# The first load of a decode kernel, split by rows: 16 rows in a load of their own, 112 behind them

## The chip, the core and the metric

The kernel runs on one core of a Trainium2 chip. The metric is the device time of one execution in microseconds, as the median of several runs: 697.33 us before the change.

## What is computed

A gated mix of two branches for one decode step: two sequences (B = 2), one token each, width D = 640. Branch a is attention over a cached K and V (32 heads, 4096 positions, 128 wide, float32), branch b a feed-forward network.

```python
def _A_ref(x, k_cache, v_cache, wq, wo):
    q = (x @ wq).reshape(B, Sq, H, Dh).transpose(0, 2, 1, 3)
    scores = einsum("bhqd,bhkd->bhqk", q, k_cache) * (Dh ** -0.5)
    p = softmax(scores, axis=-1)
    o = einsum("bhqk,bhkd->bhqd", p, v_cache)
    return o.transpose(0, 2, 1, 3).reshape(B, Sq, H * Dh) @ wo

def _B_ref(x, w1, w2):
    return silu(x @ w1) @ w2

g = sigmoid((x * gate_w).sum(-1, keepdims=True))
return g * a + (1 - g) * b
```

Everything is float32. Nearly all of the bytes are the two caches: 16 pieces of K and 16 of V, 8.39 MB each, of 298.26 MB that are read in all.

## The kernel before

**Tiling.** The 32 heads are taken four at a time, for each of the two sequences: 8 x 2 = 16 items (`items`). One item's K, and likewise its V, is 128 partitions x 16,384 floats (`SLAB`), so 65,536 bytes in each partition. Three buffers of that size hold everything big: slab a, slab b and slab v. K goes to b and a in turn (`kslab`), V to slab v, the last V to slab b.

**Per item.** VectorE and GpSimd multiply K by the query (L607 and L601), VectorE sums the products to scores (L617) and finds the peak, ScalarE takes the exponentials (L646), TensorE multiplies them with V (L697) and gathers the rows (L745).

**The start.** The queries come first. wq, 640 x 4096, is viewed as 128 rows of 20,480 floats (`wq_rows`, L274): each partition holds five rows of wq. Four of the five, 16,384 floats, go to slab a with the first load (L275), which is the load that the change touches; the fifth goes to slab v (L279). Two small loads bring x and the gate weights on ScalarE's queue (L277, L278). w1 follows into slab v (L280), and then the first K into slab b (`load_k(0)`, L286). `mm_qr` (L398) multiplies x by slab a and then by the rest in slab v. When it has read slab a, the second K is loaded into it (`load_k(1)`), and when w1 has been read, the first V into slab v.

**What sets the order.** The program is written down once as a list of operations. `Flow.dma` (L66) records a load on the queue of SP or ACT, with keys that say which part of a buffer it writes, and a semaphore of its own. `part("a")` stands for the eight keys a.0 to a.7 of slab a. An operation that reads a key waits for the last one that wrote it (`Flow.op`, L40). Loads on one queue are issued in the order in which they are recorded; in the profile they all have line L68, so they are told apart by buffer and source ("slab_a<-in_A_wq_dram" is the first load). A load waits at its issue until the readers of its buffer are done. The first four of SP's loads wait for nothing but the start.

**The end.** wo, in eight pieces of 1.31 MB, is multiplied with the attention rows (L533), two of them and w2 halfway through the items, the other six last, into slab v. The two partial sums are merged (L546, L551), copied (L841) and stored.

Of the kernel before, what the change touches and what calls it, by code (L numbers as in the profile page):

```python
# [142 lines left out]
def gated_decode(nc, x, kc, vc, wq, wo, w1, w2, gate, out):  # L143
# [14 lines left out]
    SLAB = C * DH  # L158
# [8 lines left out]
    N = len(items)  # L167
    MID = 5
    LOOPED = N - 2

    f = Flow(nc)
    V, S_, T_, G_ = nc.vector, nc.scalar, nc.tensor, nc.gpsimd

    def sb(name, shape, align=32):
        return nc.alloc_sbuf_tensor(name, shape, F32, align_bytes=align)[tuple([slice(None)] * len(shape))]
# [6 lines left out]
    slab = {n: sb(f"slab_{n}", [P, SLAB], 512) for n in "abv"}  # L182

    def part(n, *ks):
        return [f"{n}.{k}" for k in (ks or range(8))]
# [69 lines left out]
    def load_v(i):  # L255
        src = run_of(vflat, i)
        if i < N - 1:
            v_load[i] = f.dma("SP", slab["v"], src, writes=part("v"), signal=h_v if i < LOOPED else None)
            return
# [5 lines left out]
    def load_wo(grp, n, key, after):  # L265
# [6 lines left out]


    wq_rows = wq.rearrange("(p j) n -> p (j n)", j=J)  # L274
    f.dma("SP", slab["a"], wq_rows[:, :SLAB], writes=part("a"))  # L275
    xg = slab["v"][: B + 1, XG_AT : XG_AT + D]
    f.dma("ACT", xg[:B], x.rearrange("b s d -> (b s) d"), writes=part("v", 6))  # L277
    f.dma("ACT", xg[B : B + 1], gate[None, :], writes=part("v", 7))  # L278
# [5 lines left out]
        writes=part("v", 1, 2, 3, 4, 5),  # L284
# [10 lines left out]
        writes=["ident"],  # L295
# [8 lines left out]
    for q in range(Q):  # L304
# [3 lines left out]
            writes=["fold"] if q == 0 else [f"fold{q}"],  # L308
# [6 lines left out]
        writes=["sel"],  # L315
# [5 lines left out]
        writes=["half"],  # L321
# [6 lines left out]
        writes=["pick"],  # L328
# [5 lines left out]
        writes=["own"],  # L334
    )
    for q in range(Q):
# [6 lines left out]
            writes=[f"spread{q}"],  # L343
# [19 lines left out]
    for b in range(B):  # L363
# [4 lines left out]
            writes=[f"gx{b}"],  # L368
# [6 lines left out]
        writes=["ps_o"],  # L375
# [8 lines left out]
        writes=["gc"],  # L384
# [59 lines left out]
    for u in range(2):  # L444
# [10 lines left out]
            writes=[f"ps_{u}"],  # L455
# [29 lines left out]
    for src, key, k, dst, dkey, e in (  # L485
# [9 lines left out]
            writes=["turned"],  # L495
# [9 lines left out]
            writes=[ek],  # L505
# [5 lines left out]
            writes=[dkey],  # L511
        )
    for e in range(2):
# [4 lines left out]
            writes=[f"hTh{e}"],  # L518
# [93 lines left out]
    def scores(i):  # L612
        k = slab[kslab(i)].rearrange("p (c d) -> p c d", d=DH)
        for n, (c0, c1) in enumerate(((0, CV), (CV, C))):
            ops["scores", i] = f.op(
                "DVE",
                lambda c0=c0, c1=c1: V.reduce_sum(Ss[i % 2][:, c0:c1], k[:, c0:c1, :], axis=AX.X),  # L617
                reads=part(kslab(i), n),
                writes=[f"s{i % 2}{n}"],
            )  # L620
# [19 lines left out]
    def weights(i):  # L640
        s = Ss[i % 2]

        def fn():
# [16 lines left out]
            writes=["pz", "rs"],  # L660
            signal=h_e if i < LOOPED else None,
        )

    def relay(i):
        ops["relay", i] = f.op("ACT", lambda: S_.sem_inc(h_q), after=[ops["scores", i]], signal=None)
        ops["relay", i].signal = "sent"
# [59 lines left out]
    def combine(i):  # L726
# [11 lines left out]
            writes=["osb"],  # L738
            signal=h_o if i < LOOPED else None,
        )  # L740
# [37 lines left out]
    for i in range(N + 1):  # L778
        j = i - 1
        loop = j if 0 <= j < LOOPED else None  # L780

# [11 lines left out]
        if i < N:  # L793
            scores(i)
            if 1 <= i <= LOOPED:
                relay(i)
# [4 lines left out]
        if i == MID:  # L801
            after = f.users(part("a"))
            for grp in range(WO_MID):
# [5 lines left out]
                writes=part("a", 2),  # L809
# [6 lines left out]
                writes=part("a", 3),  # L816
# [72 lines left out]
```

## Time and profile before

| | |
|---|---|
| median of three runs | 697.33 us (697.23 to 697.35) |
| the profiled execution | 697.66 us |
| its span, first to last instruction | 695.7 us |
| outside the span | 1.96 us |
| bytes read | 298.26 MB, 429 GB/s over the span |
| granted TensorE clock, mean | 0.674 |

In the profile PE is TensorE's matmuls, PEld its weight loads, DVE VectorE, ACT ScalarE, POOL GpSimd, SP the sync engine, whose queue issues the big loads; "SPq" is that queue. q1 is the DMA queue of SP's loads and q10 that of ScalarE's. The DMA row gives the mean busy share of the core's 16 DMA engines in each of 40 slices, and the row below it what they moved. In a table of stretches, each row has the stretch, its length, the busy time of PE, PEld, DVE, ACT and POOL with their instruction counts, the granted clock of TensorE, the DMA share and the rate in GB/s. A packet is counted whole in the stretch in which it starts.

### The profile page before, as it was taken

Reading aid. Unit: us, or ns where it says so; the run is one execution under the profiler, and the core shown is the slowest. Engines: PE = TensorE matmul, PEld = TensorE weight load, DVE = VectorE, ACT = ScalarE, POOL = GpSimd, SP = SyncE. Lnnn points to the kernel's source line nnn. Section 1 sums busy time; section 2 is a strip of 40 time slices with the busy share of each in tenths; the row PEclk is TensorE's granted clock in tenths of the full one; section 3 lists DMA queues with packets and bytes.
Section 4 is the critical chain, followed back from the end, with each engine's and each line's share of the span. In section 5 each row is a group of like instructions: output and inputs, shape, how many; then the busy total and the mean of one; then the engine's idle time right before and its main releaser. Section 6 shows DMA issues by size and latency. Waiting matters only on the chain. (4 is left out here: it accounts for less than half of the span.)

```text
span 695.7 us, 3701 instructions
## 1 busy us (share of the span) xinstructions
PE 223.3 (32%) x1520; PEld 88.2 (13%) x1520; DVE 478.8 (69%) x235; ACT 40.1 (6%) x153; POOL 264.9 (38%) x26
## 2 busy tenths in 40 slices
PE   1630042240506053542150606041240606050377
PEld 1110011010102011110020302010120303020012
DVE  1016998969688695194949678594949588695930
ACT  0010001010101001001010101001010101001010
POOL 1006391808080624502709071533518080624400
PEclk9985556575757567877575757566575757566599
DMA  9999999999999999999999999999999999999997
GB/s 400 413 460 426 426 423 452 438 426 433 422 448 441 426 433 414 455 427 433 426 452 430 430 433 426 452 430 430 430 430 452 433 430 426 430 460 426 413 419 304
DMA packets 6938, 298.38 MB, mean 429 GB/s; under 512 B 775, under 2 KB 911, under 8 KB 1170
## 3 DMA queue, kind: packets, MB, share of 16 engines
q1 hardware_dynamic: 6924, 298.26, 99.2%
q8 instruction: 5, 0.08, 0.0%
q14 instruction: 3, 0.02, 0.0%
q10 hardware_dynamic: 6, 0.01, 0.0%
HBM read 298.26 MB, written 0.01 MB: 429 GB/s over the span
## 5 line engine op out<-in xcount | busy, mean ns | idle before, releaser
L697 PE MATMUL ps<-slab_v,pz 128*32 128x512 f32 x960 | 140.3, 745 | 352.6 <-PEq L129 326.2
L601 POOL TENSOR_TENSOR slab_b<-slab_b,qsb 128x7680 f32<-128x7680 f32 x8 | 131.4, 16421 | 204.1 <-DMA slab_b<-in_A_k_cache_dram 189.2
L601 POOL TENSOR_TENSOR slab_a<-slab_a,qsb 128x7680 f32<-128x7680 f32 x8 | 131.5, 16433 | 182.3 <-DMA slab_a<-in_A_k_cache_dram 168.9
L617 DVE TENSOR_REDUCE s<-slab_b 128x68 f32<-128x8704 f32 (+1 forms) x16 | 138.2, 8676 | 0.0
L617 DVE TENSOR_REDUCE s<-slab_a 128x68 f32<-128x8704 f32 (+1 forms) x16 | 138.1, 8675 | 0.0
L607 DVE TENSOR_TENSOR slab_b<-slab_b,ps 128x8704 f32<-128x8704 f32 x8 | 73.7, 9216 | 51.4 <-DMA slab_b<-in_A_k_cache_dram 51.4
L697 PEld LDWEIGHTS ps<-slab_v,pz 128*32 128x32 f32 x960 | 52.3, 133 | 428.2 <-issue 401.0
L607 DVE TENSOR_TENSOR slab_a<-slab_a,ps 128x8704 f32<-128x8704 f32 x8 | 73.8, 9221 | 46.5 <-DMA slab_a<-in_A_k_cache_dram 44.1
L646 ACT ACTIVATE pz<-s,nb 32x128 f32<-32x128 f32 x64 | 25.5, 398 | 581.5 <-PE ps L697 448.9
L745 PE MATMUL ps<-osb,pick 128*128 128x512 f32 x32 | 18.6, 663 | 26.9 <-PEq L129 25.1
L729 DVE SCALAR_TENSOR_TENSOR osb<-ps,rg,own 128x512 f32<-128x512 f32 x16 | 12.0, 750 | 21.0 <-PE ps L697 20.9
L757 DVE TENSOR_REDUCE row<-ps 128x128 f32<-128x512 f32 x16 | 11.1, 691 | 21.3 <-PE ps L745 21.3
L493 DVE STREAM_TRANSPOSE turned<-ps 128x416 f32<-128x416 f32 (+1 forms) x2 | 0.8, 416 | 28.4 <-PE ps L475 28.3
L418 PE MATMUL ps<-qall,spread 128*128 (+1 forms) x32 | 6.9, 300 | 25.3 <-DVE slab_b L607 24.5
L683 DVE RECIPROCAL ps<-ps 128x1 f32<-128x1 f32 x16 | 2.7, 168 | 16.4 <-PE ps L671 16.4
L533 PE MATMUL ps<-slab_v,oP 128*17 128x320 f32 (+2 forms) x128 | 12.0, 368 | 2.1 <-DMA slab_v<-in_A_wo_dram 2.1
L671 PE MATMUL ps<-rs,fold 128*128 128x1 f32 x32 | 6.0, 257 | 19.9 <-PEq L129 19.7
L398 PE MATMUL ps<-slab_a,xz 128*32 128x512 f32 x64 | 9.1, 732 | 9.3 <-DMA slab_a<-in_A_wq_dram 9.3
L646 ACT ACTIVATION_READ_ACCUMULATOR pz<-s,nb 32x1 f32 x64 | 11.8, 184 | 0.0
L533 PE MATMUL ps<-slab_a,hT 128*17 128x320 f32 x52 | 8.9, 509 | 7.0 <-DMA slab_a<-in_B_w_dram 7.0
L418 PEld LDWEIGHTS ps<-qall,spread 128*128 128x128 f32 x32 | 6.4, 206 | 33.5 <-DVE slab_b L607 24.7
L745 PEld LDWEIGHTS ps<-osb,pick 128*128 128x128 f32 x32 | 5.0, 195 | 41.1 <-issue 37.4
(70 smaller groups left out, 94.1 us busy)
## 6 DMA issues: line engine op xcount, KB each, us to landing
slab_v<-in_A_wo_dram SPq DMA_DIRECT2D x5, 1280.0 KB, 18.1
slab_v<-in_B_w_dram SPq DMA_DIRECT2D x1, 4320.0 KB, 37.3
slab_a<-in_B_w_dram SPq DMA_DIRECT2D x1, 4160.0 KB, 26.8
slab_b<-in_A_v_cache_dram SPq DMA_DIRECT2D x1, 4096.0 KB, 38.2
slab_b<-in_A_v_cache_dram SPq DMA_DIRECT2D x2, 2048.0 KB, 44.8
slab_a<-in_A_wo_dram SPq DMA_DIRECT2D x2, 1280.0 KB, 16.1
slab_v<-in_A_wq_dram SPq DMA_DIRECT2D x1, 2048.0 KB, 26.9
slab_v<-in_A_wo_dram SPq DMA_DIRECT2D x1, 960.0 KB, 25.1
```

Source lines behind the costliest of these rows:

```text
L398: last = T_.matmul(qr[u][32 * q : 32 * q + 32, :], xz[:, j, :], w[:, u * HALF : (u + 1) * HALF, q, :], start=(j == 0), stop=(j == J - 1),)
L418: return T_.matmul(ps_q[:, :DH], spread, qall.rearrange("p h b d -> p (h b) d")[:, i, :], start=True, stop=True,)
L533: last = T_.matmul(dst[32 * n : 32 * n + m, :], lhsT, w[:, n * width : (n + 1) * width], start=first, stop=final,)
L601: lambda: G_.tensor_mul(k[:, CV:, :], k[:, CV:, :], qsb[:, None, :].to_broadcast([P, C - CV, DH])),
L607: lambda: V.tensor_mul(k[:, :CV, :], k[:, :CV, :], ps_q[:, None, :DH].to_broadcast([P, CV, DH])),
L617: lambda c0=c0, c1=c1: V.reduce_sum(Ss[i % 2][:, c0:c1], k[:, c0:c1, :], axis=AX.X),
L646: last = S_.activation(pz[lo:hi, :, 4 * q : 4 * q + 4], s[lo:hi].rearrange("p (g c) -> p g c", c=4), AF.Exp, bias=nb[lo:hi], scale=SCALE, ...
L671: lambda *_: T_.matmul(ps_t[:, :1], fold.rearrange("p a q c -> p (a q c)"), rs, start=True, stop=True),
L697: last = T_.matmul(ps_v[32 * q : 32 * q + 32, :], pz[:, gr, :], v[:, gr, :], start=(gr < 4), stop=(gr >= NG - 4),)
L729: lambda: V.scalar_tensor_tensor(osb, ps_v.rearrange("p (c d) -> p c d", d=DH), rg, own[:, :, None].to_broadcast([P, 4, DH]), op0=ALU.mult ...
L745: lambda *_: T_.matmul(ps_o, pick, osb.rearrange("p c d -> p (c d)"), start=True, stop=True),
L757: lambda: V.reduce_sum(row, ps_o.rearrange("p (c d) -> p d c", d=DH), axis=AX.X),
```

## The change

```diff
@@ -167,6 +167,7 @@
     N = len(items)
     MID = 5
     LOOPED = N - 2
+    FIRST = 16
...
     wq_rows = wq.rearrange("(p j) n -> p (j n)", j=J)
-    f.dma("SP", slab["a"], wq_rows[:, :SLAB], writes=part("a"))
+    f.dma("SP", slab["a"][:FIRST], wq_rows[:FIRST, :SLAB], writes=part("a", 0))
+    f.dma("SP", slab["a"][FIRST:], wq_rows[FIRST:, :SLAB], writes=part("a", 1, 2, 3, 4, 5, 6, 7))
```

The first load is issued as two. The first of them takes partitions 0 to 15 and writes the key a.0, the second partitions 16 to 127 and writes the keys a.1 to a.7. The bytes are the same, and each partition receives the same 16,384 floats. Every reader of slab a names all eight keys, so it now waits for two semaphores instead of one; the first matmul of `mm_qr` is the first such reader. Nothing else is edited, and the lines behind the edit move down by two.

On SP's queue, at the very start of the program, the order stands like this (- before, + after; the numbers are partitions x floats of each load, in_A_wq is wq and in_B_w is w1):

```order
-L68 DMA slab_a<-in_A_wq_dram 128x16384
+L68 DMA slab_a<-in_A_wq_dram 16x16384
+L68 DMA slab_a<-in_A_wq_dram 112x16384
 L68 DMA slab_v<-in_A_wq_dram 128x4096
 L68 DMA slab_v<-in_B_w_dram 128x8640
```

One row became two, and the loads behind them each stand one place later. No other engine's order differs, but for the line numbers.

## The prediction

> **What bounds the kernel now.** I read the slices of the page first, then the queues, the chain that ended last, SP's own waits, and last the stretches of the start. The slices and the queues say that the loads set the time:
>
> ```profile
> span 695.7 us, 3701 instructions
> PE 223.3 (32%) x1520; PEld 88.2 (13%) x1520; DVE 478.8 (69%) x235; ACT 40.1 (6%) x153; POOL 264.9 (38%) x26
> DMA  9999999999999999999999999999999999999997
> GB/s 400 413 460 426 426 423 452 438 426 433 422 448 441 426 433 414 455 427 433 426 452 430 430 433 426 452 430 430 430 430 452 433 430 426 430 460 426 413 419 304
> q1 hardware_dynamic: 6924, 298.26, 99.2%
> ```
>
> No compute engine is busy for more than 69% of the span, while the packets of SP's queue (q1) fill 99.2% of what 16 DMA engines could give. There is no slice in the middle with a gap. The stretches put a price on that:
>
> ```profile
> 0.00:22.00 22.00, 2.94 (x12) 2.77 (x12) 2.93 (x22) 1.46 (x2) 2.07 (x10) 1.00 0.93 386
> 22.00:672.00 650.00, 205.02 (x1354) 79.93 (x1354) 473.53 (x208) 38.25 (x150) 262.83 (x16) 0.65 1.00 434
> 672.00:692.00 20.00, 14.04 (x122) 4.60 (x123) 2.02 (x4) 0.42 (x1) 0.00 (x0) 1.00 0.94 398
> 692.00:695.70 3.70, 1.30 (x36) 0.94 (x32) 0.33 (x1) 0.00 (x0) 0.00 (x0) 1.00 0.01 3
> ```
>
> The last two columns are the mean share of the DMA engines and GB/s. From 22 to 672 us the share is 1.00 at 434 GB/s, that is 434 / 16 = 27.1 GB/s for each engine. The chain that ended last fits this: its long pieces are loads.
>
> ```profile
> 626.01 28.87 DMA slab_v<-in_A_v_cache_dram
> ...
> 666.28 23.28 DMA slab_v<-in_A_wo_dram
> ...
> 691.08 2.25 PE ps L533 x56
> ```
>
> The queue never runs dry because SP issues well ahead, and its long waits are for free buffers:
>
> ```profile
> SPq L68 <- PE ps L697: 485.2, 14, 39.3
> SPq L68 <- PE ps L398: 29.8, 1, 29.8
> ```
>
> So a microsecond that all DMA engines lose at the start has nowhere to be made up. It moves the end by about a microsecond, and a microsecond won there is won at the end.
>
> **The start, round by round.** The first load is 128 rows of 65,536 bytes. The queue's line for the first 21.75 us shows 128 packets and 8.39 MB, so one packet is one row and each of the 16 engines brings eight rows. The second fence has the stretches, the wait for the first packet and then the rounds (last two columns as above):
>
> ```profile
> q1 hardware_dynamic: 128, 8.39, 93.0%
> ```
>
> ```profile
> 0.00:1.70 1.70, 0.00 (x0) 0.00 (x0) 0.67 (x7) 0.13 (x1) 0.94 (x8) 1.00 0.01 3
> 1.70:4.80 3.10, 0.00 (x0) 0.00 (x0) 1.20 (x9) 1.16 (x1) 1.13 (x3) 1.00 1.06 338
> 4.80:7.20 2.40, 0.00 (x0) 0.00 (x0) 0.00 (x0) 0.00 (x0) 0.00 (x0) 1.00 1.01 437
> 7.20:9.65 2.45, 0.00 (x0) 0.00 (x0) 0.00 (x0) 0.00 (x0) 0.00 (x0) 1.00 0.99 429
> ...
> 16.90:19.31 2.41, 0.00 (x0) 0.00 (x0) 0.00 (x0) 0.00 (x0) 0.00 (x0) 1.00 1.00 435
> ```
>
> The timeline has the issues of SP's queue and the first matmul that reads the load (start, length, and in brackets the idle time before it):
>
> ```profile
> 0.74 0.39 SPq L68 DMA_DIRECT2D slab_a<-in_A_wq_dram  x1
> 1.20 0.41 SPq L68 DMA_DIRECT2D slab_v<-in_A_wq_dram  x1
> 1.65 0.46 SPq L68 DMA_DIRECT2D slab_v<-in_B_w_dram  x1
> 2.14 0.50 SPq L68 DMA_DIRECT2D slab_b<-in_A_k_cache_dram  x1
> 23.27 9.10 PE L398 MATMUL ps<-slab_a,xz 128*32 128x512 f32 x64 [9.31 <-DMA slab_a<-in_A_wq_dram]
> ```
>
> Packets begin 1.70 us into the span, 0.96 us after the first issue. The first round takes 3.10 us and each later one 2.41. Whatever the change can win lies in that first round and ahead of it.
>
> **The change, part by part.**
>
> *One more issue on SP.* The first load becomes two, and everything behind is issued one issue later, by 0.46 us (0.74 to 1.20). The load behind them is needed only when the eight rounds are done, at about 21.7 us, and its issue moves from 1.20 to about 1.66. The second part's own issue comes at 1.20; with the same 0.96 us its rows are ready at 2.16, before the first round ends at 4.80. Price: nothing. Without that cover it would be 0.46 us.
>
> *One more wait on TensorE.* The first matmul on slab a (L398) now waits for two loads. It waits already, 9.31 us, and behind it stand the release of slab a and the load issued at 32.44. That load's turn comes only after the first K load, which lands 56.1 us after its issue at 2.14, at 58.2:
>
> ```profile
> slab_b<-in_A_k_cache_dram SPq DMA_DIRECT2D x1, 56.1
> 32.44 0.33 SPq L68 DMA_DIRECT2D slab_a<-in_A_k_cache_dram  x1
> ```
>
> So it stands in the queue 58.2 - 32.44 = 25.8 us before its turn. If the rows of slab a land later, the K load behind them lands later too, and most of that margin stays. Price: nothing.
>
> *The ramp.* With one row for each engine in the first load, the first round may start more together. It can win at most what the round exceeds the others by, 3.10 - 2.41 = 0.69 us, and if the issue shrinks too, the 0.96 us ahead of the packets: 1.65 us in all. From the other side it wins nothing. I take 0.69 as the round's excess, and count it as hidden where the round is long anyway.
>
> *Where the 16 rows land.* All big loads of before write 128 rows at once, and there 16 engines run at 434 GB/s. The change's first load writes rows 0 to 15, side by side. No row of this trace shows 16 engines that write into 16 neighbouring partitions. Sixteen engines serve 128 partitions, eight to an engine. If the way into the buffer is also one for every eight partitions, at one engine's 27.1 GB/s, engines that write into the same eight have to share it. The bounds: with 16 ways reached, the round stays at 2.41 us; if each eight are neighbours, 16 rows reach two ways, and the load takes eight rounds instead of one, 7 x 2.41 = 16.9 us more. Between them stand eight ways (pairs of neighbours; one round more) and four ways (fours; three rounds more). The full rate was seen only where each engine had its own eight partitions (no round over 2.45 us after the first), which speaks for a way of its own for every eight, so I go to the side of sharing; but two ways is an end, so I take four, 3 x 2.41 = 7.2 us. That choice is the weakest step. [...]
>
> *The 112 rows behind them.* They are seven rows for each engine, rows 16 to 127. In before, eight rows for an engine gave no collision at all (2.41 us in every round). Blocks of seven don't fall on groups of eight or four, so in most rounds some ways are asked by two engines and others by none. Bounds: no collision, 0; every row meets another one, seven rounds doubled, 7 x 2.41 = 16.9 us. I take half, 8.4 us, for the slowest engine, which is the one that sets when a load has landed, and stays behind since each engine's later share is fixed. [...]
>
> *Sum.* 7.2 + 8.4 = 15.6 us, less 0.69 for the ramp that lies inside the longer first load: 14.9. The profiled execution took 697.66 us (its span of 695.7 and 1.96 around it), 0.33 over the median of 697.33. 697.66 + 14.9 = 712.6, and less 0.33: **712.2 us**. Without collisions behind the first part it is 697.3 + 7.2 - 0.7 = 703.8; with all of them 697.3 + 7.2 + 16.9 - 0.7 = 720.7.
>
> **The rivals.**
>
> *Neighbours don't share.* The 16 rows go at the full rate, as the second round does (437 GB/s), and the sevens as well. Then only the ramp is left: between nothing and 0.69 us, so 696.6 to 697.3, say 697.0. For it: the trace shows one rate, 27.1 GB/s per engine, and an engine's own limit explains it without any port. Against it: that rate was only seen with all 128 partitions in play. It decides at the first load's landing: near 5 us here, near 11 in the forecast. Chance 0.16.
>
> *Engines belong to partitions.* The change wouldn't do what it says: the 16 rows go to those engines that serve their partitions, a few rows each, and the others start on the second part at once. If the second part is dealt out by partition too, each engine still has eight rows, and the time is 697.3. Chance 0.08. If instead the sevens go to all engines, four engines bring 4 + 7 = 11 rows, three more than now, 7.2 us or more: 704.5, inside the forecast's range, and counted there.
>
> *The ramp and the issue shrink together.* A load with one row for each engine starts sooner and runs its round at 2.41 us: 1.65 us less, 695.7. For it: the first round is slow by 0.69 us, and 0.96 us pass ahead of it. Against it: an issue of 0.39 us stands in that, and nothing shows that the rest depends on the number of rows. Over 1.4 us has to be won for this to count as faster. Chance 0.08.
>
> **How the numbers follow.** A measurement of this kernel can tell about 0.2% from no change, 1.4 us here (its three runs lie within 0.12 us). The forecast, sharing, has 0.68, with its own range of 703.8 to 719, just inside the worst case of 720.7. The rivals without sharing have 0.16 + 0.08 = 0.24 within 0.2%, and 0.08 are faster. To hold 8 in 10 the range must reach down to the unchanged time and the ramp's gain: 696.5 to 719. Slower 0.68, same 0.24, faster 0.08.
>
> **What would show it.** In the profile after, the first 12 us decide. If the first load's rows share ways, the first 16 packets end near 11 us rather than 5, the rate in the stretch from 1.70 to 11 us is far under 430 GB/s, and "DMA slab_a" releases L398 well after 30 us instead of 23.27. If the sevens collide, the rate from 11 to 30 us is also under 434, and the DMA share falls in the last slices, as the engines end far apart. The middle should be unchanged at 434 GB/s with share 1.00 on the slowest engines. The forecast is wrong if the second round still begins near 4.8 us; it is wrong in size if the landing of the first load is late by less than 7 us, or the end is late by more or less than the start.

## The result, and the profile after

The change makes the kernel slower: 718.69 us median of six runs (717.59 to 721.06) against 697.31 us (697.09 to 697.40), a ratio of 1.0313 (95% interval 1.0303 to 1.0323). That is 21.4 us, where 14.9 were forecast. The direction was right and the size too small: the median lies 0.3 us below the upper end of the stated range, 719, and the ratio applied to the 697.33 us that the forecast started from gives 719.2, just above it. The profiled execution took 718.40 us with a span of 716.5, 20.7 and 20.8 us more than before.

The page of the changed kernel has the span, the slices and the queue:

```profile
span 716.5 us, 3703 instructions
DMA  9999999999999999999999999999999999999996
GB/s 176 238 353 462 413 454 422 424 454 413 454 424 435 440 421 454 399 467 414 446 428 432 443 421 450 424 439 432 429 446 421 446 428 432 439 428 446 413 417 280
q1 hardware_dynamic: 6940, 298.26, 99.1%
```

The bytes are the same 298.26 MB. The DMA engines are as busy as before, but in the first three slices of 17.9 us they move 176, 238 and 353 GB/s, with a 9 for the share in each. So the packets did not start later, they lasted longer. The stretches behind the start show that nothing else changed (length, busy times, clock, DMA share, GB/s):

```profile
0.00:45.00 45.00, 3.67 (x16) 2.97 (x20) 2.93 (x22) 1.46 (x2) 2.07 (x10) 1.00 0.96 220
85.00:655.00 570.00, 173.54 (x1072) 68.45 (x1072) 434.59 (x182) 33.35 (x135) 240.04 (x15) 0.63 1.00 434
```

From 85 to 655 us the rate is 434 GB/s, as before. The whole difference is there when the first load has landed, which the first matmul on slab a shows in the timeline:

```profile
0.74 0.86 SPq L68 DMA_DIRECT2D slab_a<-in_A_wq_dram  x2
1.65 0.75 SPq L68 DMA_DIRECT2D slab_v<-in_A_wq_dram  x1
44.27 8.76 PE L400 MATMUL ps<-slab_a,xz 128*32 128x512 f32 x64 [28.21 <-DMA slab_a<-in_A_wq_dram]
```

It starts at 44.27 instead of 23.27 us, 21.0 us later, and the end is 20.8 us later. The next stretches go round by round. Each row starts where the first packet of a round does, and ends where that of the next begins (the last row: where its own first packet ends). The first row holds the 16 rows that go first, the others the seven rounds behind them:

```profile
1.77:9.39 7.62, 0.00 (x0) 0.00 (x0) 1.13 (x9) 1.10 (x1) 1.06 (x3) 1.00 1.12 138
9.39:15.31 5.92, 2.36 (x10) 2.27 (x10) 0.46 (x4) 0.00 (x0) 0.00 (x0) 1.00 0.92 178
15.31:20.08 4.77, 0.59 (x2) 0.50 (x2) 0.61 (x4) 0.17 (x1) 0.00 (x0) 1.00 1.04 234
20.08:23.29 3.21, 0.00 (x0) 0.00 (x0) 0.00 (x0) 0.00 (x0) 0.00 (x0) 1.00 0.92 306
23.29:26.93 3.64, 0.00 (x0) 0.00 (x0) 0.00 (x0) 0.00 (x0) 0.00 (x0) 1.00 1.10 306
26.93:30.97 4.04, 0.00 (x0) 0.00 (x0) 0.00 (x0) 0.00 (x0) 0.00 (x0) 1.00 1.11 260
30.97:35.71 4.74, 0.00 (x0) 0.00 (x0) 0.00 (x0) 0.00 (x0) 0.00 (x0) 1.00 0.92 207
35.71:40.38 4.67, 0.00 (x0) 0.00 (x0) 0.00 (x0) 0.00 (x0) 0.00 (x0) 1.00 0.97 228
```

The first 16 rows took 7.62 us where the first round of before took 3.10, and the seven rounds 30.99 us instead of 7 x 2.41 = 16.9. In both traces the first matmul on slab a starts behind the last packet of slab a (22.95 and then 23.27 us before, 43.24 and then 44.27 after), so the shares are told by last packets, from the packet records of the two traces. The last one of the first round ends at 11.34 us instead of 6.04: 5.3 us belong to the 16 rows. The last one of slab a ends at 43.24 instead of 22.95, 20.3 us late: 20.3 - 5.3 = 15.0 us belong to the 112 rows. The rest of the 21.0 us passes between the last packet and the first matmul, 1.03 us instead of 0.32; why is open. The larger part of the loss is thus in the load that looks almost like the old one.

### The profile page after: what moved, and what is told of

It reads as the page before. It is cut to its first block, busy times and chain, and to the rows that moved or that the text cites. A ratio compares the mean times of both kernels' runs of the same rounds, so it can differ in the third digit from the quotient of the medians.

```text
span 716.5 us, 3703 instructions
## 1 busy us (share of the span) xinstructions
PE 224.8 (31%) x1520; PEld 86.3 (12%) x1520; DVE 478.9 (67%) x235; ACT 40.1 (6%) x153; POOL 264.9 (37%) x26
## 3 DMA queue, kind: packets, MB, share of 16 engines
q1 hardware_dynamic: 6940, 298.26, 99.1%
HBM read 298.26 MB, written 0.01 MB: 416 GB/s over the span
## 5 line engine op out<-in xcount | busy, mean ns | idle before, releaser
L699 PEld LDWEIGHTS ps<-slab_v,pz 128*32 128x32 f32 x960 | 49.8, 134 | 429.4 <-issue 401.9
L731 DVE SCALAR_TENSOR_TENSOR osb<-ps,rg,own 128x512 f32<-128x512 f32 x16 | 12.0, 750 | 20.7 <-PE ps L699 20.7
## 6 DMA issues: line engine op xcount, KB each, us to landing
slab_v<-in_A_wo_dram SPq DMA_DIRECT2D x5, 1280.0 KB, 17.9
```

What stands on the lines that cost most here:

```text
L699: last = T_.matmul(ps_v[32 * q : 32 * q + 32, :], pz[:, gr, :], v[:, gr, :], start=(gr < 4), stop=(gr >= NG - 4),)
L731: lambda: V.scalar_tensor_tensor(osb, ps_v.rearrange("p (c d) -> p c d", d=DH), rg, own[:, :, None].to_broadcast([P, 4, DH]), op0=ALU.mult ...
```

## The experiments

The theory, the author's own: 16 engines that write at the same time into partitions with a common way into the buffer slow each other down, so the destination's partitions set the time (*shared ways*). A trace shows how long a round takes, not a way. Rivals: the source rows in memory, the number and shortness of the loads, and the start of the program. In all edits below the rest of the kernel is as before. Those with a loop of loads, and the split in the middle, also let the kernel's `plan` look at loads with a shared semaphore last when it decides which waits to write; the halves, the split at the other end and the runs with 48 and 32 rows lack this line and lose as much. Each of the runs other than the columns stands for one execution, beside before at 697.46 to 697.63 us. The six runs of the change lie 3.5 us apart, so smaller differences between two single executions mean nothing.

**Destination or source: four ways to cut the load into eight.** Eight loads of 16 rows, where each side is either 16 neighbours or 16 rows eight apart:

```diff
-    f.dma("SP", slab["a"], wq_rows[:, :SLAB], writes=part("a"))
+    for r in range(8):
+        f.dma("SP", slab["a"][DST], wq_rows[SRC, :SLAB], writes=part("a", r))
```

with DST and SRC each `16 * r : 16 * r + 16` (block) or `r:P:8` (stride). If the destination decides, stride from block takes as long as stride into stride, and block from stride as long as block into block; if the source decides, it is the other way round. Block into block:

> The first load as eight loads of 16 neighbouring rows into 16 neighbouring partitions; all data as before. Shared ways into the buffer (the destination sets it): each of the eight goes like the first load of the change, 8.9 us a round against 2.41, so about 8 x 8.9 - 20 = 51 us over before, 748 us. Neighbouring rows of the source (the memory that is read sets it): the same 748. Many small loads as such: the same 748, and then the three runs beside it as well.

Measured: 751.95 us. Stride into stride:

> Eight loads of 16 rows that lie eight apart, into partitions eight apart; all data as before. [...] Source rows: they are far apart, no cost, 697 to 698. Many small loads: 748 as with neighbouring rows.

Measured: 718.49 us. Stride from block:

> Eight loads of 16 neighbouring rows of the source into partitions eight apart. The partitions get each other's rows of wq, so the queries are others and only the time counts. [...] Source rows: 748 us, as with blocks on both sides.

Measured: 718.35 us. Block from stride:

> Eight loads of source rows eight apart into 16 neighbouring partitions; again the partitions get each other's rows of wq, and only the time counts. Shared ways: 748 us, as with blocks on both sides. Source rows: 697 to 698 us if distance in the source is what matters.

Measured: 751.38 us. The two with blocks in the buffer agree within 0.6 us, the two with strides in the buffer within 0.2, whatever was read; between the pairs lie 33 us. The destination decides, the source rows do not. All four have eight loads, so their number has no part in the 33 us; that it doesn't make the 21 us of the strides either, the halves below show, which lose as much with two loads. Nor do ways of eight neighbouring partitions each, one end of what the prediction allowed for, fit the runs: rows eight apart would then never meet, and the strides cost 21 us. Rounds of block from stride, then of stride from block:

```profile
9.43:18.59 9.16, 2.95 (x12) 2.77 (x12) 1.07 (x7) 0.17 (x1) 0.00 (x0) 1.00 0.95 108
18.59:27.79 9.20, 0.00 (x0) 0.00 (x0) 0.00 (x0) 0.00 (x0) 0.00 (x0) 1.00 1.00 114
```

```profile
6.77:11.88 5.11, 2.60 (x12) 2.52 (x12) 0.57 (x4) 0.00 (x0) 0.00 (x0) 1.00 1.00 205
11.88:17.00 5.12, 0.35 (x2) 0.26 (x2) 0.51 (x3) 0.17 (x1) 0.00 (x0) 1.00 1.06 218
```

One round, 1.05 MB, takes 9.2 us into 16 neighbours (114 GB/s) and 5.1 us into 16 partitions eight apart (205 GB/s).

**How the 112 rows are dealt.** The second load as seven loads of 16 rows, seven apart:

```diff
-    f.dma("SP", slab["a"][FIRST:], wq_rows[FIRST:, :SLAB], writes=part("a", 1, 2, 3, 4, 5, 6, 7))
+    for t in range(7):
+        f.dma("SP", slab["a"][16 + t : P : 7], wq_rows[16 + t : P : 7, :SLAB], writes=part("a", 1 + t))
```

> The change with its second load dealt by hand: seven loads of 16 rows that lie seven apart, so that engine e gets row 16 + 7e + t in load t. If a load of 112 rows gives each engine seven neighbouring rows and its cost comes from which partitions are written at the same time, this is the same traffic and the same time as the change, 717 to 721 us, with the same rounds. If the cost comes from something else in a load of 112 rows, such as seven rows an engine, the seven loads cost less or more: 697 + 5 = 702 us where they collide with nothing.

Measured: 718.91 us, the time of the change. In the trace the median packets of its eight rounds last 8.6, 5.4, 4.8, 3.0, 3.7, 4.6, 4.7 and 4.4 us; those of the change 8.7, 5.3, 4.8, 3.0, 3.6, 4.5, 4.6 and 4.4. So a load of 112 rows behaves as if each engine got seven neighbouring rows.

**The same seven loads in another order** (`for t in (2, 3, 0, 1, 4, 5, 6)`). If the 112 rows of the change are dealt as these loads deal them, its short rounds, the third and fourth behind the 16 rows (3.21 and 3.64 us), are those of the sets of partitions that start at 18 and 19:

> The seven loads dealt by hand in another order: the sets of partitions that start at 18 and at 19 go first, then those at 16, 17, 20, 21, 22. [...] If the set of partitions makes a round short, the two short rounds now come right behind the first load, medians near 3 to 3.7 us, and the other five take 4.4 to 5.4 us; the total stays at 717 to 721 us. If it is the time since the start, the third and fourth round stay the short ones.

Measured: 720.56 us. The first four rounds behind the 16 rows:

```profile
9.63:14.20 4.57, 2.15 (x10) 2.15 (x10) 0.00 (x0) 0.00 (x0) 0.00 (x0) 1.00 0.95 244
14.20:17.73 3.53, 0.80 (x3) 0.63 (x3) 1.07 (x7) 0.17 (x1) 0.00 (x0) 1.00 1.06 297
17.73:21.90 4.17, 0.00 (x0) 0.00 (x0) 0.00 (x0) 0.00 (x0) 0.00 (x0) 1.00 1.08 251
21.90:26.66 4.76, 0.00 (x0) 0.00 (x0) 0.00 (x0) 0.00 (x0) 0.00 (x0) 1.00 1.00 220
```

The third and fourth are short no longer (4.17 and 4.76 instead of 3.21 and 3.64), and the set that starts at 19 took its short round along (3.53). The one at 18 did so only in part: 4.57 in the place where the change has 5.92, with a median packet of 4.06 us where 3 to 3.7 were expected. It overlaps with the slow first load. So the set of partitions makes the round, mixed with what goes ahead of it.

**Halves.** `slab["a"][:64]` and `slab["a"][64:]`:

> The first load in two halves, partitions 0 to 63 and 64 to 127. [...] If only loads of few rows are slow (four rows an engine here), 698 to 702 us.

Measured: 718.38 us, rounds as with the strides:

```profile
6.64:11.76 5.12, 0.00 (x0) 0.00 (x0) 0.00 (x0) 0.00 (x0) 0.00 (x0) 1.00 1.00 205
```

Four rows an engine, and the loss is the same. It is not the narrow load that costs but the partitions it reaches.

**The split at the other end.** `slab["a"][:112]`, then `slab["a"][112:]`:

> The split at the other end: 112 rows first, the last 16 behind them. Shared ways: seven rounds of 3.2 to 4.7 us and one of 8.9, the same sum as the change, 716 to 721 us. If the cost lies in what is first (the start of the queue, the memory's first use), the 112 rows take it and the 16 rows, no longer first, run at about 2.4 us: 705 to 712 us.

Measured: 717.81 us. The first rounds and the last, the 16 rows:

```profile
1.77:5.45 3.68, 0.00 (x0) 0.00 (x0) 1.13 (x9) 1.10 (x1) 1.07 (x3) 1.00 1.05 249
5.45:10.19 4.74, 0.00 (x0) 0.00 (x0) 0.00 (x0) 0.00 (x0) 0.00 (x0) 1.00 0.96 221
...
29.95:37.42 7.47, 0.00 (x0) 0.00 (x0) 0.00 (x0) 0.00 (x0) 0.00 (x0) 1.00 1.13 140
```

The 16 rows are as slow at the end of the load (7.47 us) as at its start (7.62).

**The split in the middle of the kernel.** The first load whole, and the K load of item 4 split instead; the two products that read it wait for both parts:

```diff
     def load_k(i):
         n = kslab(i)
+        if i == 4:
+            after = f.users(part(n))
+            f.dma("SP", slab[n][:16], run_of(kflat, i)[:16], writes=part(n))
+            f.dma("SP", slab[n][16:], run_of(kflat, i)[16:], writes=["rest"], after=after)
+            return
```

> The first load whole as before; instead the K load of the fifth item, in the middle of the first half, is split into 16 and 112 rows. Shared ways: the engines lose the same time there as at the start, since the queue has no gap to make it up: about 20 us over before, 716 to 719 us. If the loss belongs to the start of the program, or if the slack of the buffers takes it up in the middle: 697 to 700 us.

Measured: 719.37 us. Three stretches there, the 16 rows and the first two rounds behind them:

```profile
172.31:180.16 7.85, 1.74 (x12) 0.52 (x16) 7.85 (x2) 0.00 (x0) 0.00 (x0) 0.50 1.09 142
180.16:185.60 5.44, 5.44 (x48) 1.67 (x44) 2.48 (x5) 0.00 (x0) 0.00 (x0) 0.80 0.94 193
185.60:190.35 4.75, 3.48 (x26) 1.30 (x18) 1.55 (x3) 2.23 (x9) 0.00 (x0) 1.00 0.93 207
```

The loss, 21.9 us, is the same 170 us into the program, and no slack takes it up.

**The control: split by columns.**

```diff
-    f.dma("SP", slab["a"], wq_rows[:, :SLAB], writes=part("a"))
+    FIRST = 2048
+    f.dma("SP", slab["a"][:, :FIRST], wq_rows[:, :FIRST], writes=part("a", 0))
+    f.dma("SP", slab["a"][:, FIRST:], wq_rows[:, FIRST:SLAB], writes=part("a", 1, 2, 3, 4, 5, 6, 7))
```

> The first load split by columns: 128 partitions x 2,048 floats first, then the other 14,336 columns. All partitions are in play in both, so shared ways cost nothing; one more issue and one more wait are as in the change. Shared ways: 696.5 to 698, the ramp's 0.69 us at most won. If the split itself costs (the second issue, the second wait), 698 to 719.

Measured: 697.24 us median of 11 runs against 697.48 of 15, a ratio of 0.9998 (0.9989 to 1.0007): no difference. The first matmul on slab a:

```profile
22.69 9.17 PE L400 MATMUL ps<-slab_a,xz 128*32 128x512 f32 x64 [13.71 <-DMA slab_a<-in_A_wq_dram]
```

It starts 0.58 us earlier than in before. Two loads instead of one, the second issue and the second wait cost nothing that shows, and nothing that is clear of the noise is won at the end either.

**Who pays: some of the engines, or all.** 48 and 32 rows first, with the edit of the change and another `FIRST`:

> The change with 48 rows first (three for each engine) and 80 behind them (five). [...]

> The change with 32 rows first (two for each engine) and 96 behind them (six). [...]

Measured: 726.09 us with 48 rows and 717.25 with 32. Rounds two to four with 48, then the second and third with 32:

```profile
8.26:16.50 8.24, 0.00 (x0) 0.00 (x0) 0.00 (x0) 0.00 (x0) 0.00 (x0) 1.00 1.01 127
16.50:24.86 8.36, 0.00 (x0) 0.00 (x0) 0.00 (x0) 0.00 (x0) 0.00 (x0) 1.00 1.04 134
24.86:30.07 5.21, 2.36 (x10) 2.27 (x10) 0.38 (x3) 0.00 (x0) 0.00 (x0) 1.00 0.89 189
```

```profile
6.29:11.43 5.14, 0.00 (x0) 0.00 (x0) 0.00 (x0) 0.00 (x0) 0.00 (x0) 1.00 1.06 217
11.43:16.16 4.73, 2.36 (x10) 2.27 (x10) 0.24 (x2) 0.00 (x0) 0.00 (x0) 1.00 1.02 222
```

If only some of the engines paid, the packets of the others would take the 2.4 us of before. None does: with 48 rows all 16 packets last 6.0 us or more in each of the first load's rounds and 4.5 or more in each of the five behind them, and with 32 rows all 16 last 4.1 us or more in each of the eight rounds. So all pay; which engines meet in a round, no run shows. The two rounds of 8.2 and 8.4 us with 48 rows are longer than the 5.1 of the strides, with as many rows in a round. From the first packet to the end of the first packet of the last round, the eight rounds with 48 took 6.5 + 8.2 + 8.4 + 24.9 = 48.0 us, 28.0 over the 20.0 of before, against 28.5 measured at the end.

## Why the prediction was off

**Right.** The bound (the queue has no gap, so what the engines lose at the start comes back at the end): 21.0 us at the first matmul, 20.8 at the end, and about the same loss, 21.9, for a split in the middle of the kernel. The issue and the wait at nothing: the columns show it. That neighbours in the buffer cost time: a round takes 9.2 us into blocks and 5.1 into strides, whatever was read. That they share ways, four engines to one, is the author's explanation; no run shows a way. The first load: three rounds more less the ramp, 7.2 - 0.69 = 6.5 us, were forecast, 5.3 measured. The factor of four came out nearly right, 9.2 us a round being 3.8 times 2.41, but it was a choice between two bounds that nothing in the trace of before had shown, so it was partly luck.

**The step that failed** is the term for the 112 rows: "I take half, 8.4 us, for the slowest engine". It measured 15.0, nearly the upper bound of 16.9. Half would hold if only engines that meet on a way paid, each in half of the rounds, 3.5 x 2.41 = 8.4 us; that was the author's estimate, and no run shows which engines meet. In the trace no packet of the 112 rows takes the 2.4 us of before: all 16 last 4.1 us or more in five of the seven rounds, and 2.8 or more in the other two. The rounds last 4.0 to 5.9 us in the five, 3.2 and 3.6 in the two. With 15.0 for 8.4 the prediction's sum is 697.3 + 7.2 + 15.0 - 0.7 = 718.8 us, against 718.69 measured. That it comes so close is luck in part: the term for the first load is 1.2 us too large, and the 0.7 us behind the last packet stand in no term.

**Also wrong:** that the engines would end far apart and the last slices show it. In the trace the first packets of the first K load began within 1.7 us of each other before (36.8 to 38.6 us) and within 2.3 after (56.4 to 58.7). So the engines stayed together through the slow rounds. That each engine's later share is fixed, from which the prediction had them stay behind, is not shown.

**The rivals.** "Neighbours don't share" is refuted by the first 7.62 us. "Engines belong to partitions" is refuted by the trace and the dealing of sevens: the 16 packets of the first load run side by side from 2.5 to 9.4 us, and no packet of the 112 rows starts before 9.39 us, although under this rival the other engines would have begun them at once; and the 112 rows behave as seven to an engine. "The ramp and the issue shrink together" can't be seen in the change, where the ramp is buried; the columns, with all partitions in play, won 0.24 us, inside their interval.

**What the ramp is** stays open, as does which engines meet in a round, and why all 16 pay.

## What to carry to other kernels

Cut a load by columns, not by partitions: the two loads of all 128 partitions that were tried cost nothing, while two halves, 16 + 112 rows and every other cut by rows that was tried lost 19.6 us or more for 8.39 MB here. In a kernel whose DMA queue has no gap, price a change of a load by rounds, so many rows for each engine by the time of one, and ask which partitions the 16 engines write in the same round. Take the round's time from a measured round into such partitions, and for all 16 engines, not as an average over some of them: in the change no packet of the 16 or the 112 rows kept to the 2.4 us of before. Two of its rounds were shorter than the others, 3.2 and 3.6 us.

## What the runs showed of the hardware that was not expected

- A round of 16 rows of 65,536 bytes takes 2.41 us in the load of all 128 rows. In loads cut by rows it took 4.7 to 5.1 us (halves, strides, 32 rows first), 8.2 to 8.4 (the second and third round with 48 rows first) and 9.2 to 9.3 (blocks): about 2, 3.4 and 3.8 times 2.41.
- In the run with 32 rows first, the second round of the 32 neighbours takes 5.14 us, and the first two rounds behind them 4.73 and 5.11. In the two short rounds of the change two packets take 4.4 to 4.6 us and the other 14 only 2.8 to 3.8.
- While the rate halves, the DMA share stays near 1: in the first 45 us of the change it is 0.96 at 220 GB/s, and 1.00 at 434 from 85 to 655 us. A DMA row full of nines does not say that the engines move what they can: read the GB/s row beside it.
